# A build-time instruction plan that looks further along the product list, and counts waits in full from an earlier stage on

## The chip, the core and the metric

The kernel runs on one core of a Trainium2 chip. A core has TensorE (matrix products, "PE" in a profile; its weight loads are shown apart as "PEld"), VectorE ("DVE"), ScalarE ("ACT"), GpSimd ("POOL") and SyncE ("SP", which here only issues transfers), all reading one on-chip memory (SBUF); TensorE writes to eight accumulation banks (PSUM), from which VectorE and ScalarE fetch the results. The metric is the device time of one execution in microseconds, as a median of several runs.

## The reference, cut to what matters

A transformer block with linear attention and a gated feed-forward part, on 2048 tokens of width 1024, bf16 in and out:

```python
def _A_ref(x, wqkv, wo):                       # H = 32 heads of width 32
    q, k, v = split(x @ wqkv)
    phi = lambda t: jnp.where(t > 0, t + 1, jnp.exp(t)) + 1e-6
    pq, pk = phi(q), phi(k)
    kv = jnp.einsum("bhsd,bhse->bhde", pk, v)
    z = jnp.einsum("bhsd->bhd", pk)
    num = jnp.einsum("bhqd,bhde->bhqe", pq, kv)
    den = jnp.einsum("bhqd,bhd->bhq", pq, z)[..., None] + 1e-6
    return merge_heads(num / den) @ wo

def _B_ref(x, W_gate, W_up, W_down):           # F = 3584
    gate = x @ W_gate
    up = x @ W_up
    return (gate * (gate > 0) * up) @ W_down

h = x + _A_ref(_layernorm(x), wqkv, wo)
out = h + _B_ref(_layernorm(h), W_gate, W_up, W_down)
```

## The kernel before

Every large product is cut into quadrants and done with seven products in place of eight (Strassen-Winograd), so each has sums of inputs ahead of it and sums of results after it. `Quad` is one such group; its seven products are `p1` to `p7`, in the Q, K and V stages four matmuls of 128x512 each. `A`, `D` and `E` are PSUM banks.

```python
class Quad:
    def p1(self):
        self.A, self.D, self.E = self.banks()
        self.prod(self.A, 1, True)
        self.fork(self.D, self.A)                 # ScalarE copies the bank A to the bank D
    def p6(self):
        self.prod(self.A, 6, False)
        self.u2 = self.snap(self.A, 0)            # ScalarE copies A to SBUF
    def p5(self):
        self.prod(self.E, 5, True)
    def p7(self):
        self.prod(self.A, 7, False)
        self.u3 = self.snap(self.A, 1)
    def p2(self):
        self.prod(self.D, 2, False)
        self.out["c22"](self.E, self.u3)          # VectorE: E + u3; E is then free for p3
        self.out["c11"](self.D)
    def p4(self):
        self.prod(self.A, 4, False)
        self.out["c21"](self.A)
    def p3(self):
        self.prod(self.E, 3, False)
        self.out["c12"](self.E, self.u2)
```

In the Q and K stages a result goes through phi. `direct` takes a bank, `add` the sum of a bank and a copy, and `join2` ends the two sums together:

```python
        def direct(dst, k):
            def f(ps):
                nc.scalar.activation(out=e[:, k, :], in_=ps, func=ACT.Exp)
                phi_clamp(e[:, k, :])             # VectorE tensor_scalar, SBUF to SBUF
                phi_join(dst, ps, e[:, k, :])     # VectorE scalar_tensor_tensor, reads PSUM
            return f
        def add(k):
            return lambda E, u: nc.vector.tensor_tensor(out=c[:, k, :], in0=E, in1=u, op=ALU.add)
```

The attention of a tile of 128 tokens. `nd01` is groups 0 and 1, `nd2` group 2; all take turns on three PSUM banks (5, 6, 7), and so does `wo`:

```python
att = [ring_of([bank(b) for b in (5, 6, 7)])]
...
        def group(self, g):
            ...                                   # n = 3 or 2 heads' groups
            ps = att[0]()
            for k in range(n):
                nc.tensor.matmul(ps[:, k * NDW:(k + 1) * NDW], ...)        # 128x132
            ... nc.scalar.activation(Ln) ... nc.scalar.activation(Exp) ...
            nc.vector.tensor_tensor(out=self.o[...], in0=ndv[...], in1=rd[...], op=ALU.mult)
            if g == 2:
                self.oT = oT_ring()
                nc.sync.dma_start_transpose(out=self.oT, in_=self.o)
        def wo(self, j):
            ps = att[0]()
            for c in range(KC):                   # 8 matmuls of 128x512
                nc.tensor.matmul(ps, lhsT=self.oT[:, c, :], rhs=wo_sb[:, c, js], ...)
            nc.vector.scalar_tensor_tensor(out=self.h[:, js], in0=ps, ..., accum_out=self.acc[:, j:j + 1])
            if j == 1:
                return self.square                # then a ScalarE square, Ln, Exp, and
                                                  # nc.gpsimd.tensor_scalar(...) on 128x1024 of SBUF
```

The sums of the inputs of the gate and up products (VectorE, SBUF to SBUF, 128x1024) and of the left operand are work in the background:

```python
            return [sub(t[1], b[0][1], b[0][0]), sub(t[0], b[1][1], t[1]),
                    sub(t[2], b[1][1], b[0][1]), sub(t[3], b[1][0], t[0])]        # GW.sums
        return [tt(s1, a21, a22, ALU.add), tt(s2, s1, a11, ALU.subtract),
                tt(s4, a12, s2, ALU.subtract), tt(s3, a11, a21, ALU.subtract)]    # left_sums
```

None of this goes straight to the chip. `Plan` records every operation as a node (a run of matmuls into one bank is one node), works out what each depends on, and puts every engine's nodes in an order by a simulation at build time with its own estimates. `nom` is a TensorE node's place in the product list, in ns of TensorE work ahead of it; `late` is by when a node should start. The engines then run their lists strictly in the order that came out. The core of it:

```python
    WINDOW = 6000.0
    MIXED = (120000.0, 215000.0)                  # ns of the plan's own clock
    def schedule(self):
        ...
                if e == "tensor":
                    while first < len(pe) and pe[first] in done:
                        first += 1
                    limit = nodes[pe[first]].nom + self.WINDOW
                    a = [i for i in a if nodes[i].nom <= limit]
                s = max(clock[e], min(nodes[i].ready for i in a))
                if best is None or s < best[0]:
                    best = (s, e, a)
            ...
            s, e, a = best
            now = [i for i in a if nodes[i].ready <= s]
            i = min(now, key=lambda i: (nodes[i].nom if e == "tensor" else nodes[i].late, i))
            v = nodes[i]
            if e != "tensor":
                wait = (1.2 if self.MIXED[0] < s < self.MIXED[1] else 0.5) * v.hold
                soon = [j for j in a if s < nodes[j].ready < s + wait and nodes[j].late < v.late - 1500.0]
                if soon:
                    i = min(soon, key=lambda j: (nodes[j].late, j))
                    v = nodes[i]
                    s = v.ready
```

Of the kernel before, what the change touches and what calls it, by code (L numbers as in the profile page):

```python
# [32 lines left out]
class Plan:  # L33
# [3 lines left out]

    G = 64
    SEM = 100.0
    WINDOW = 6000.0  # L40
    AHEAD = 120000.0
    OPENING = 45000.0
    MIXED = (120000.0, 215000.0)

    class Node:
        __slots__ = ("eng", "calls", "preds", "hold", "lat", "open", "dma", "late", "ready", "left", "start", "nom")
# [156 lines left out]
    def schedule(self):  # L203
# [14 lines left out]
        while True:  # L218
            best = None
            for e in engines:  # L220
# [8 lines left out]
# [5 lines that stand above are left out]
# [11 lines left out]
# [4 lines that stand above are left out]
# [1325 lines left out]
```

## Time and profile before

| | before |
|---|---|
| time, median of 3 runs | 724.11 us (724.1 to 725.8) |
| profiled span | 722.2 us |
| TensorE busy | 713.6 us, 99% of the span |
| VectorE busy | 569.0 us, 79% |
| ScalarE busy | 277.9 us, 38% |
| GpSimd busy | 56.5 us, 8% |
| TensorE clock granted | 0.999 |

The stages, by the trace: to some 60 us the inputs, their norm and the first K and V groups; to 115 us the other K and V groups; to 200 us the Q groups, into which from 139 us the first half's attention and output projection are woven; to 285 us the first gate and up groups with the second half's attention; to 568 us the gate and up groups alone; then the down projection. The line number of nearly every instruction in the profile is 123, since the plan records and issues all of them from one place: an instruction is told by engine, operation and size. A matmul's busy time in the profile overlaps that of the next, so a row of matmuls without a gap shows as wholly busy, and short gaps hide in the overlap.

### The profile page before, as it was taken

What the parts mean: (1) busy time and instruction counts of PE and PEld (TensorE: products, weight loads), DVE (VectorE), ACT (ScalarE), POOL (GpSimd) and SP (SyncE); (2) the same over time, 40 slices, a digit from 0 to 9 for tenths busy, and PEclk for the clock granted to TensorE, in tenths of its full rate; (3) what the DMA queues carried; (4) which work ended last, traced back from release to release, by engine and by line L of the source; (5) the groups of instructions that cost most, each with busy time, mean ns of one, the idle gap of its engine ahead of it and who ended that gap; (6) DMA issues with size and microseconds to landing.
All of it is one profiled execution on the core that took longest, in us unless ns stands there. A gap on an engine that the chain in (4) does not pass through costs nothing.

```text
span 722.2 us, 11197 instructions
## 1 busy us (share of the span) xinstructions
PE 713.6 (99%) x4163; PEld 396.1 (55%) x4163; DVE 569.0 (79%) x966; ACT 277.9 (38%) x548; POOL 56.5 (8%) x62
## 2 busy tenths in 40 slices
PE   8999999999999999999999999999999999999998
PEld 3444445444454444444444444444444688888887
DVE  7899655888797975666766968769768879899996
ACT  5887555665655443333333333333333220001100
POOL 0000000012102120000000000000000004001452
PEclk9999999999999999999999999999999999999999
DMA  9556407069846630547145584685591878777974
GB/s 295 153 97 139 147 0 215 20 110 209 216 94 154 138 88 8 145 118 196 59 142 173 173 257 131 205 262 181 169 298 59 275 269 200 222 262 239 247 76 59
DMA packets 156503, 117.40 MB, mean 163 GB/s; under 512 B 54944, under 2 KB 140192, under 8 KB 156320
## 3 DMA queue, kind: packets, MB, share of 16 engines
q1 hardware_dynamic: 148832, 113.01, 54.1%
q0 software_dynamic: 7616, 3.67, 4.9%
q8 instruction: 32, 0.52, 0.3%
q14 instruction: 23, 0.19, 0.1%
HBM read 70.52 MB, written 34.08 MB: 145 GB/s over the span
## 4 chain that ended last, share of the span: by engine, by line
PE 87%; DVE 6%; ACT 3%; DMA 2%; issue 1%; SPq 0%; DVEq 0%; ACTq 0%
PE psum L123 87%; DVE mem L123 5%; ACT mem L123 2%; DMA mem<-mem 2%; DMA mem<-in_A_wqkv_dram 1%; DVE tiny L123 1%; ACT tiny L123 1%; SPq L123 0%; ACT psum L123 0%; DVEq L123 0%; ACTq L123 0%
## 5 line engine op out<-in xcount | busy, mean ns | idle before, releaser
L123 PE MATMUL psum<-mem 128*128 128x512 bf16 (+4 forms) x4147 | 712.7, 335 | 5.1 <-DVE mem L123 2.1
L123 PEld LDWEIGHTS <-mem 128*128 128x128 f16 (+1 forms) x4163 | 396.1, 98 | 322.4 <-issue 8.0
L123 DVE TENSOR_TENSOR mem<-psum,mem 128x512 f32<-128x512 f32 (+2 forms) x240 | 187.2, 793 | 97.3 <-ACT mem L123 64.7
L123 DVE TENSOR_TENSOR mem<-mem 128x512 f16<-128x512 bf16 (+8 forms) x400 | 241.2, 643 | 8.7 <-DMA mem<-mem 3.0
L123 ACT COPY mem<-psum 128x512 f32<-128x512 f32 (+2 forms) x124 | 92.7, 749 | 211.6 <-PE psum L123 205.5
L123 ACT COPY psum<-psum 128x512 f32<-128x512 f32 (+1 forms) x68 | 49.1, 722 | 157.8 <-PE psum L123 157.8
L123 POOL DMA_DIRECT2D out_dram<-mem x28 | 34.1, 1300 | 412.1 <-DVE mem L123 412.0
L123 ACT ACTIVATE mem<-psum 128x512 bf16<-128x512 f32 x90 | 53.5, 597 | 19.8 <-PE psum L123 19.2
L123 DVE SCALAR_TENSOR_TENSOR mem<-mem 128x512 bf16<-128x512 bf16 (+1 forms) x71 | 57.7, 812 | 1.2
L123 DVE SCALAR_TENSOR_TENSOR mem<-psum,mem 128x512 bf16<-128x512 f32 x66 | 45.4, 689 | 14.8 <-PE psum L123 12.5
L123 POOL TENSOR_SCALAR mem<-mem,tiny 128x1024 bf16<-128x1024 bf16 x16 | 20.7, 1296 | 243.0 <-ACT tiny L123 243.0
L123 ACT ACTIVATE mem<-mem,tiny 128x1024 bf16<-128x1024 bf16 x24 | 27.5, 1145 | 5.2 <-DVE tiny L123 5.0
L123 DVE TENSOR_SCALAR mem<-mem 128x512 bf16<-128x512 bf16 (+1 forms) x49 | 16.6, 340 | 15.3 <-ACT mem L123 15.1
L123 ACT ACTIVATE tiny<-tiny 128x1 f32<-128x1 f32 (+2 forms) x120 | 23.9, 205 | 7.5 <-DVE tiny L123 4.5
L123 ACT ACTIVATE mem<-mem 128x1024 bf16<-128x1024 f32 (+1 forms) x23 | 24.3, 1057 | 4.5 <-DVE mem L123 3.1
L123 DVE TENSOR_TENSOR mem<-psum,tiny 128x384 bf16<-128x384 f32 (+1 forms) x48 | 22.8, 507 | 4.1 <-ACT tiny L123 3.5
L123 ACT ACTIVATE tiny<-psum 128x12 f32<-128x12 f32 (+1 forms) x48 | 8.0, 170 | 18.5 <-PE psum L123 17.8
L123 DVE BATCH_NORM_STATS2 tiny<-mem 128x6 f32<-128x512 bf16 x16 | 10.3, 680 | 2.4 <-DMA mem<-in_A_x_dram 2.4
L123 ACT CAST mem<-psum 128x512 bf16<-128x512 f32 x18 | 10.3, 581 | 3.5 <-PE psum L123 3.2
L123 DVE TENSOR_SCALAR mem<-mem,tiny 128x1024 bf16<-128x1024 bf16 x16 | 8.6, 540 | 3.4 <-ACT tiny L123 3.3
L123 ACT ACTIVATION_READ_ACCUMULATOR mem<-mem,tiny 128x1 f32 x24 | 4.5, 188 | 0.0
L123 DVE TENSOR_SCALAR tiny<-tiny 128x1 f32<-128x1 f32 x16 | 3.4, 210 | 0.4
(17 smaller groups left out, 12.2 us busy)
## 6 DMA issues: line engine op xcount, KB each, us to landing
l_dram<-mem SPq DMA_DIRECT2D x98, 128.0 KB, 2.4
mem<-l_dram SPq DMA_DIRECT2D x12, 896.0 KB, 6.5
mem<-in_A_x_dram SPq DMA_DIRECT2D x32, 256.0 KB, 3.2
mem<-in_B_W_up_dram SPq DMA_DIRECT2D x14, 512.0 KB, 5.4
mem<-in_B_W_gate_dram SPq DMA_DIRECT2D x14, 512.0 KB, 4.4
mem<-in_B_W_down_dram SPq DMA_DIRECT2D x28, 256.0 KB, 3.5
r_dram<-mem SPq DMA_DIRECT2D x56, 128.0 KB, 2.4
mem<-r_dram SPq DMA_DIRECT2D x8, 896.0 KB, 5.3
```

The lines of the kernel that those rows point to most:

```text
L123: call = lambda: getattr(getattr(self.nc, eng), op)(*args, **k)
```

## The change

Two constants of the plan. `WINDOW` is how far beyond the first product not yet done TensorE may look for one that is ready, and `MIXED` the stretch of the plan's clock in which VectorE, ScalarE, GpSimd and SyncE may leave their engine waiting up to 1.2 times the length of the operation at hand (0.5 times elsewhere) when a more urgent one is about to be ready. The first is to find products that fill TensorE's waits, the second is to let urgent evictions go first in the K and V stage too. No operation is added, removed or changed; only the orders differ.

```diff
     G = 64
     SEM = 100.0
-    WINDOW = 6000.0
+    WINDOW = 10000.0
     AHEAD = 120000.0
     OPENING = 45000.0
-    MIXED = (120000.0, 215000.0)
+    MIXED = (62000.0, 215000.0)
```

Built, the two programs have the same 4163 matmuls. What the orders show, in the names above:

- VectorE, from the earlier start of `MIXED` alone: in four K groups the sum `c22` (E + u3) comes ahead of the `c11` join, not behind it; in the group at 82 us it also comes ahead of two `left_sums`; two or three more neighbours swap. TensorE's order doesn't change from this.
- TensorE, from `WINDOW` alone, output projection stage: before, each round is `wo` (8 matmuls), `nd2` (2), `wo` (8), `nd01` (6), one product of a Q group (4). After, one Q product is put ahead of the first `wo`, so that each round has the Q product that stood one round later, and the last of them (`p4`) no longer stands between the last `wo` pairs. VectorE's work follows: the 128x1024 `sub`s of `GW.sums`, one in each of four rounds before, begin two rounds later.
- TensorE, from `WINDOW`, at 205 us: `p5` of the second gate/up half group and `p3` of the first come ahead of `p6` of the second. And at 570 us, in the first group of the down projection, `p1` of its second half comes ahead of `p1` of its first half.
- A few transfers and background sums from 400 us on change places.

## The prediction

> **What bounds the kernel now.** I read the page's busy times first, then busy times by stage, then the list of TensorE's waits, and last the timeline around each wait.
>
> ```profile
> span 722.2 us, 11197 instructions
> ...
> PE 713.6 (99%) x4163; PEld 396.1 (55%) x4163; DVE 569.0 (79%) x966; ACT 277.9 (38%) x548; POOL 56.5 (8%) x62
> ...
> L123 PE MATMUL psum<-mem 128*128 128x512 bf16 (+4 forms) x4147 | 712.7, 335 | 5.1 <-DVE mem L123 2.1
> ```
>
> TensorE is the bound, and only 5.1 us of idle time stand before its matmuls. But the 335 ns are overlapped records, so I need the true pitch. By stage (columns: stretch, its length, then busy time and count by engine):
>
> ```profile
> 147.00:183.00 36.00, 34.49 (x193) 16.75 (x191) 29.07 (x70) 20.30 (x71) 7.16 (x6) 1.00 0.85 176
> ...
> 285.00:560.00 275.00, 275.00 (x1276) 124.48 (x1274) 202.35 (x347) 92.06 (x115) 0.00 (x0) 1.00 0.56 169
> ```
>
> From 285 to 560 us there are 1276 matmuls of 128x512 in 275 us: 215.5 ns each, and no wait. A single record of that size lasts 380 ns. So whenever the timeline shows TensorE idle for g before a matmul, g + (0.380 - 0.216) = g + 0.16 us is lost; a gap under 0.16 doesn't show at all. Its waits:
>
> ```profile
> PE psum L123 <- DVE mem L123: 2.1, 5, 0.9
> ...
> PE psum L123 <- DMA mem<-mem: 0.8, 1, 0.8
> ...
> PE psum L123 <- ACT psum L123: 0.2, 1, 0.2
> ```
>
> I went through the start of every matmul in the trace and summed what goes beyond its pitch. Up to 60 us it is 3.7 us (warm-up and first inputs; no order changes there). From 60 us on the whole of it is 4.1 us, in twelve gaps: 0.07 at 67.3, 0.32 at 68.5, 0.55 at 82.1, 0.14 at 147.4, 0.94 at 149.6, 0.21 at 164.2, 0.51 at 169.4, 0.51 at 174.7, 0.16 at 192.3, 0.39 at 205.6, 0.20 at 267.4, and 0.10 at 572.6 hidden in the overlap. That is the most an order can bring: 4.1 of 724 us, 0.6%. The change can't reach 2% on the fast side.
>
> **What the Trainium skill says.** "TensorE: Matmul & The Clock Gate", "Step-by-step: what each phase is for", gives the back-to-back gap as N/2.4 GHz plus about 2.5 ns, 216 ns at N=512; the trace agrees (215.5). "Perfetto Trace Analysis", "Tensor Engine Instruction (MATMUL, LD_WEIGHTS)", says the end of a matmul is an estimate and that ScalarE, VectorE and GpSimd are strict FIFOs; hence the gaps from starts, and hence an eviction stuck behind whatever VectorE's list has ahead of it. "SBUF — State Buffer", "SBUF: two separate sides", says that a VectorE operation with two SBUF inputs and a GpSimd operation lock each other out of a shared port for a whole instruction. The trace agrees: the same 128x1024 sub takes 1.15 us at 162.3, 167.6 and 172.9, each time over a GpSimd operation of 1.19 us, and 0.68 us at 175.7 without one.
>
> **The change part by part.** No operation is added or removed, so the sum is over gaps alone.
>
> *K stage, from the earlier start of the full waits.* VectorE's order ahead of the gap at 82.1:
>
> ```profile
> 78.95 1.56 DVE L123 TENSOR_TENSOR mem<-mem 128x512 f16<-128x512 bf16 x4 [1.70 <-DMA mem<-mem]
> 80.42 0.29 DVE L123 TENSOR_SCALAR mem<-mem 128x512 bf16<-128x512 bf16 x1
> 80.75 0.69 DVE L123 SCALAR_TENSOR_TENSOR mem<-psum,mem 128x512 bf16<-128x512 f32 x1
> 81.36 0.68 DVE L123 TENSOR_TENSOR mem<-psum,mem 128x512 f32<-128x512 f32 x1
> ```
>
> ```profile
> 82.09 1.24 PE L123 MATMUL psum<-mem 128*128 128x512 bf16 x5 [0.38 <-DVE mem L123]
> ```
>
> The last VectorE line is c22, which frees E for p3. The new order puts it ahead of the join (0.69) and of two or three of the four sums (about 0.39 each). Its other input, the copy u3, is done at 80.60 (ScalarE, 80.02 + 0.58), so it can run from 80.65 to 81.33; p3 was due at 82.09 - 0.55 = 81.54. The gap goes: -0.55. At 68.5 the same swap moves c22 from 67.79 up to about 67.36 (u3 is done at 67.30): it ends at 68.04, p3 is due at 68.20: -0.32. From 83 to 147 us TensorE has no wait, and what is moved back (left sums that the next group needs from 90 us on) has over 4 us to spare, so nothing gives this back. Part sum -0.87.
>
> *The gap at 149.6.* TensorE waits for the DMA transpose of the first attention tile:
>
> ```profile
> 149.57 19.52 PE L123 MATMUL psum<-mem 128*128 128x512 bf16 x112 [0.78 <-DMA mem<-mem]
> ```
>
> A Q product of 4 x 0.216 = 0.86 us goes into this gap of 0.94. It needs only the fork of its bank (ScalarE, done at 147.85), so it starts at 148.63 and ends at 149.49: -0.86, paid out at 181.7, where the product then is no longer in the way.
>
> *The gaps at 164.2, 169.4, 174.7.* Each `wo` takes the bank of the `wo` before it, and waits for that eviction:
>
> ```profile
> 172.33 1.19 POOL L123 TENSOR_SCALAR mem<-mem,tiny 128x1024 bf16<-128x1024 bf16 x1 [4.09 <-ACT tiny L123]
> 172.57 0.42 DVE L123 TENSOR_TENSOR mem<-psum,tiny 128x256 bf16<-128x256 f32 x1 [0.45 <-ACT tiny L123]
> 172.91 1.15 DVE L123 TENSOR_TENSOR mem<-mem 128x1024 f16<-128x1024 bf16 x1
> ...
> 173.99 0.68 DVE L123 SCALAR_TENSOR_TENSOR mem<-psum,mem 128x512 bf16<-128x512 f32 x1
> ...
> 174.72 7.62 PE L123 MATMUL psum<-mem 128*128 128x512 bf16 x36 [0.34 <-DVE mem L123]
> ```
>
> The product in the bank was done at about 173.17, but VectorE had begun a background sub, stretched to 1.15 by GpSimd, and evicts only at 173.99. In the new order the first such sub comes two rounds later: the gaps at 164.2 and 169.4 (0.21 and 0.51) go. Ahead of the `wo` now at 174.7 the sub is there again, with a 1.22 us join before it, so a gap of 0.2 (as at its first time before) to 0.5 stays: I put 0.35. After that `wo` follows `wo`, whose banks were free long before, and no sub is in the way. Part sum 1.23 - 0.35 = -0.88. Against it: with the last Q product gone from 181.7, the last `wo` pair starts 5.2 us after the group it needs (1.73 x 3), and the way there was 1.7 us (group to transpose issue at 178.31) plus 3.1 to 3.5 (median to landing, and the longest near it): +0.1.
>
> *The gap at 205.6.* p6 waits for ScalarE's fork, which stood behind a Relu:
>
> ```profile
> 204.42 0.60 ACT L123 ACTIVATE mem<-psum 128x512 bf16<-128x512 f32 x1 [0.34 <-DVE mem L123]
> ...
> 204.92 0.59 ACT L123 COPY psum<-psum 128x512 f32<-128x512 f32 x1
> ...
> 205.56 7.65 PE L123 MATMUL psum<-mem 128*128 128x512 f16 x42 [0.23 <-ACT psum L123]
> ```
>
> p5 needs the Relu alone (205.02), and was due at 205.17. But p3, now next at 206.03, needs two small sums that end near 206.1 to 206.2: -0.25 of the 0.39. At 572.6 the half product put ahead takes the hidden gap: -0.1. The gaps at 147.4, 192.3 and 267.4 stay: the last two come from VectorE behind a GpSimd operation, which moves with them.
>
> Sum: -0.87 - 0.86 - 0.88 + 0.1 - 0.25 - 0.1 = -2.86 us. I take 0.25 off for gaps that I don't see: -2.6, so 721.5 us.
>
> **Rivals.** (1) VectorE bounds the output projection, and the filled gap comes back as longer waits: 29.07 of 36 us busy from 147 to 183. For it speaks that every wait there but one ends with VectorE; against it that VectorE itself idles 7 us there, and that the moved work finds lighter rounds. Then the 0.86 and much of the 0.88 are lost: about 723.2. (2) The urgent-first waits leave VectorE idle in the K stage and push sums or the norm late, so that a later group's p6 or p5 waits: VectorE is busy 31.3 of 40 us from 60 to 100, and the moved sums are due 4 us later, so I give this little; it would make 723.5 to 724.5. (3) The transfers and sums that change places from 400 us on open a new gap in the last stage, where VectorE has 19.8 of 20 us busy from 660 to 700 and TensorE waits for nothing only because all of it comes just in time: one load that is late by its whole way (5.3 to 6.5 us median to landing for the large ones) would make 727. Speaks against it: none of TensorE's products after 590 us moves, and only neighbours swap.
>
> **Range and chances.** All gaps gone but none new: 720.7. Only the K stage and half of the rest: 722.9. The before's own runs reach 1.7 above their median, so I widen up: 720.6 to 723.3. For 2% it would have to be under 709.6 or over 738.6: the first is out of reach, the second takes a new stall of 14 us.
>
> **What would show it.** Starts of p3 without a gap at 68 and at about 81.5; no idle before a Q product at 148.6; TensorE's idle after DVE down from 2.1 to about 1.2 (0.9 at 29 us, and one gap left ahead of the `wo` now at 174.7); p5 at about 202.5 (205.2 less the gain) and at its pitch; as many matmuls by 285 as before, 2.7 us earlier; no wait at all after. Wrong if gaps near 160 to 180 sum to over 1 us still, or if TensorE waits for a transfer after 560 us.

## Result, and the profile after

| | before | changed | ratio, with its 95% interval |
|---|---|---|---|
| time, median, first comparison | 724.23 us (723.78 to 725.8, 6 runs) | 722.27 us (721.18 to 723.02, 6 runs) | 0.9968 (0.9955 to 0.9981) |
| time, median, second comparison | 724.49 us (724.09 to 724.97, 10 runs) | 722.01 us (721.55 to 722.77, 6 runs) | 0.9967 (0.9955 to 0.9979) |
| profiled span | 722.2 us | 719.9 and 720.1 us | |

The change takes 0.3% off: 0.0032 x 724.23 = 2.3 us, with an interval of 1.4 to 3.3 us. (The ratio is that of the means; the medians differ by 1.96 us in the first comparison and by 2.48 in the second.) That is far under 2%, and the 722.27 us lie within the predicted 720.6 to 723.3. The page of the changed kernel (span; then busy time, share of the span and count by engine):

```profile
span 719.9 us, 11145 instructions
...
PE 710.4 (99%) x4112; PEld 396.6 (55%) x4163; DVE 568.1 (79%) x966; ACT 278.2 (39%) x548; POOL 57.3 (8%) x62
```

Busy times outside TensorE are within 1 us of those of before (VectorE 568.1 for 569.0); no operation was changed, so what can have changed is TensorE's waits. One trap stands in the PE figure: x4112. The kernel has 4163 matmuls, as the weight loads (PEld x4163) show, so 51 records are missing from this trace. Each leaves a false gap of one pitch, 0.215 us, in front of the next matmul. I leave those out below. A second profile of the same kernel has all 4163, and I use it where counts matter. Its TensorE from 66 to 183 us (start, length, operation, count; the timeline begins a new line where TensorE was idle):

```profile
65.73 117.56 PE L123 MATMUL psum<-mem 128*128 128x512 bf16 x646
```

One line. In the kernel before, the same stretch has six, broken at 68.52, 82.09, 149.57, 169.44 and 174.72. Its busy times by stage (stretch, length, busy time and count of PE, PEld, DVE, ACT, POOL; granted clock, DMA share, GB/s):

```profile
60.00:100.00 40.00, 40.00 (x232) 19.98 (x230) 31.98 (x58) 26.53 (x52) 0.00 (x0) 1.00 0.47 112
147.00:183.00 36.00, 35.90 (x201) 17.63 (x201) 29.51 (x72) 21.53 (x70) 7.16 (x6) 1.00 0.85 184
```

From 147 to 183 us TensorE does 201 matmuls where it did 193: 8 x 0.2155 = 1.72 us. VectorE's busy time there rose only from 29.07 to 29.51. And TensorE's waits in the first profile of the changed kernel (us in total, times, longest):

```profile
PE psum L123 <- DVE mem L123: 1.1, 1, 1.1
PE psum L123 <- ACT mem L123: 0.7, 1, 0.7
```

Against before: the wait for a DMA (0.8) and the one for ScalarE's bank copy (0.2) are gone, and of five waits for VectorE (2.1 us) one is left, the one near 29 us, where the order didn't change; shorter ones hide in the overlap or stand under "issue".

As in the prediction, I took the start of every matmul and summed what goes beyond its pitch, place by place (us lost, at the time of before; "again" is the second profile of the changed kernel; the last column belongs to an experiment below):

| place | before | changed | changed, again | `MIXED` to 300000 |
|---|---|---|---|---|
| 67.3 | 0.07 | 0.07 | 0.07 | 0.07 |
| 68.5, K stage | 0.32 | 0 | 0 | 0 |
| 82.1, K stage | 0.55 | 0 | 0 | 0 |
| 147.4 | 0.14 | 0.14 | 0.14 | 0.14 |
| 149.6, transpose | 0.94 | 0.07 | 0.06 | 0 |
| 164.2, `wo` | 0.21 | 0 | 0 | 0 |
| 169.4, `wo` | 0.51 | 0 | 0 | 0 |
| 174.7, `wo` | 0.51 | 0.27 | 0.27 | 0.27 |
| 181, last `wo` pair | 0 | 0 | 0 | 0.08 |
| 192.3 | 0.16 | 0 | 0.36 | 0 |
| 205.6 | 0.39 | 0.20 | 0.20 | 0.20 |
| 213.6, `nd2` (new) | 0 | 0.29 | 0.21 | 0 |
| 267.4 | 0.20 | 0.20 | 0.21 | 0 |
| 572.6 | 0.10 | 0.10 | 0.10 | 0.10 |
| sum | 4.10 | 1.34 | 1.61 | 0.85 |

The orders win 2.76 us in one profile and 2.49 in the other. Of this the spans show 2.3 and 2.1: up to 60 us, where the order is the same, the changed kernel's profiles lose 4.19 and 4.18 us and that of before 3.78. The account is complete: the span less the loss before 60 us and the loss after it is 714.3 to 714.4 us in the profile of before and in all ten others below, so nothing but these gaps makes the spans differ. I come back to the opening under what I hadn't expected.

The main gaps, line by line, in the first profile of the changed kernel. VectorE near 81 us (timeline: start, length, operation; in brackets idle time and what ended it):

```profile
79.87 0.29 DVE L123 TENSOR_SCALAR mem<-mem 128x512 bf16<-128x512 bf16 x1
80.72 0.69 DVE L123 TENSOR_TENSOR mem<-psum,mem 128x512 f32<-128x512 f32 x1 [0.56 <-ACT mem L123]
81.32 0.68 DVE L123 SCALAR_TENSOR_TENSOR mem<-psum,mem 128x512 bf16<-128x512 f32 x1
```

The second line is `c22`. VectorE now waits 0.56 us for the copy that `c22` needs, and does the join afterwards. `c22` starts at 80.72 where it started at 81.36, so the bank for `p3` is free in time. That idle 0.56 us is the meaning of "counts waits in full".

The `wo` at 173 us (same view; the last line is TensorE's weight load for it):

```profile
170.90 1.19 POOL L123 TENSOR_SCALAR mem<-mem,tiny 128x1024 bf16<-128x1024 bf16 x1 [3.59 <-ACT tiny L123]
...
171.48 1.15 DVE L123 TENSOR_TENSOR mem<-mem 128x1024 f16<-128x1024 bf16 x1
...
172.56 0.68 DVE L123 SCALAR_TENSOR_TENSOR mem<-psum,mem 128x512 bf16<-128x512 f32 x1
...
173.30 0.74 PEld L123 LDWEIGHTS <-mem 128*128 128x128 bf16 x4 [0.38 <-issue]
```

The pattern of before in its one place left: a background `sub` of 1.15 us stretched over GpSimd's 1.19, the eviction behind it, and the `wo` behind the eviction, 0.27 us late.

And the gap that no step of the prediction had, at 213.6 us:

```profile
211.69 0.69 DVE L123 SCALAR_TENSOR_TENSOR mem<-mem 128x512 bf16<-128x512 bf16 x1
212.29 0.69 DVE L123 TENSOR_TENSOR mem<-mem 128x1024 f16<-128x1024 bf16 x1
...
212.89 0.69 DVE L123 SCALAR_TENSOR_TENSOR mem<-psum,mem 128x512 bf16<-128x512 f32 x1
...
213.64 1.29 PEld L123 LDWEIGHTS <-mem 128*128 128x128 bf16 x8 [0.41 <-issue]
```

`nd2` needs the bank of a `wo` whose product ends at 212.30. At 212.29 VectorE had just begun a background `sub`; the eviction comes 0.6 us later, and `nd2` starts at its end.

### The profile page after: what moved, and what is told of

The parts are those of the page before. It is cut to its first block, busy times and chain, and to the rows that moved or that the text cites. A ratio compares the mean times of both kernels' runs of the same rounds, so it can differ in the third digit from the quotient of the medians.

```text
span 719.9 us, 11145 instructions
## 1 busy us (share of the span) xinstructions
PE 710.4 (99%) x4112; PEld 396.6 (55%) x4163; DVE 568.1 (79%) x966; ACT 278.2 (39%) x548; POOL 57.3 (8%) x62
## 4 chain that ended last, share of the span: by engine, by line
PE 94%; DVE 3%; DMA 2%; issue 1%; ACT 0%; SPq 0%; DVEq 0%; ACTq 0%
PE psum L123 94%; DVE mem L123 2%; DMA mem<-in_A_wqkv_dram 1%; DMA mem<-mem 1%; SPq L123 0%; DVE tiny L123 0%; ACT mem L123 0%; ACT tiny L123 0%; DVEq L123 0%; ACTq L123 0%
```

## The experiments

My theory: the gain is the sum of the gaps that each constant closes, the two parts are independent, and what is left (173, 213.6, 265 us) is VectorE having begun something else when an urgent eviction came due. Rivals: the waits cost something elsewhere in the K stage; the moves of the window after 200 us undo part of its gain; GpSimd has nothing to do with the gap at 173. In each diff the left side is the kernel named.

**1. The waits alone (against before).**

```diff
-    MIXED = (120000.0, 215000.0)
+    MIXED = (62000.0, 215000.0)
```

> The early start of the full waits alone (WINDOW back at 6000). My theory, that the two parts add: the gaps at 68.5 and 82.1 us (0.32 and 0.55 before) are gone as in the changed kernel, all later ones stay as before (0.94 at 149, 0.21, 0.51 and 0.51 from 163 to 175, 0.39 at 205), TensorE loses 4.10 - 0.87 = 3.2 us after 60 us, ratio 0.9988. The rival, that VectorE's waiting is paid for later: the same two gaps are gone but a new one of some 0.5 to 0.9 us opens by 115 us, ratio 1.000.

Measured: ratio 0.9984 (0.9977 to 0.9991), 723.81 against 724.73 us. TensorE's waits in its profile:

```profile
PE psum L123 <- DVE mem L123: 1.4, 3, 0.7
...
PE psum L123 <- DMA mem<-mem: 0.8, 1, 0.8
...
PE psum L123 <- ACT psum L123: 0.2, 1, 0.2
```

Five waits for VectorE became three; the other two stand as before. By the matmul starts the gaps at 68.5 and 82.1 are gone, all others are within 0.01 us of before, and none is new: 4.10 to 3.23 us, 0.87 as the prediction worked out. The rival of sums pushed late in the K stage falls.

**2. The window alone (against before).**

```diff
-    WINDOW = 6000.0
+    WINDOW = 10000.0
```

> WINDOW 10000 alone (full waits from 120000 again). My theory: gaps of 0.32 and 0.55 at 68 and 82 us as before; 149.6 falls from 0.94 to 0.07, 164 and 169 go, about 0.27 is left near 174, 205 falls from 0.39 to 0.20, and the new 0.29 near 214 is there, since it comes from this part: 4.10 - 1.9 = 2.2 us lost after 60 us, ratio 0.9974. The rival, that the window's gain needs the earlier K stage (the two don't add): about half, with longer gaps near 164 to 175, ratio 0.9985.

Measured: 0.9978 (0.9969 to 0.9987), 723.27 us. The gaps of the K stage are there (0.32 and 0.54), and the changed kernel's gaps after it: 0.08 at 150.1, 0.26 at 174.3, 0.20 at 205.0, 0.17 at 214.7; 0.19 stands at 191.1. Sum 2.27 us, so 1.83 of the 4.10 are won. Both parts together: 0.87 + 1.83 = 2.70 us of gaps, against 2.76 and 2.49 for the whole change; 0.0016 + 0.0022 = 0.0038 by the ratios, against 0.0032 with an interval that holds it. The parts add up. The new gap belongs to the window.

**3. The full waits also after 215000 (against the changed kernel).** The new gap looks like those that the full waits removed in the K stage, so I let them go on.

```diff
-    MIXED = (62000.0, 215000.0)
+    MIXED = (62000.0, 300000.0)
```

> The changed kernel with the full waits kept up to 300000 of the plan's clock in place of 215000. Theory: the new gap of 0.29 us at 213.6 and the 0.20 at 265.0 are evictions and sums for freed banks that stand behind background sums of 128x1024, because the full waits end just ahead of them; with the waits kept on, both go and nothing else moves: 1.34 - 0.49 = 0.85 us lost after 60 us, ratio to before 0.9962 to 0.9953. Rival: the gaps come from GpSimd's hold on the shared port or from the moved products, and are still there (sum over 0.4 us), ratio as the changed kernel, 0.9968.

Measured: 0.9952 (0.9940 to 0.9965), 721.44 us. VectorE at the place of the new gap:

```profile
211.55 0.69 DVE L123 TENSOR_TENSOR mem<-mem 128x1024 f16<-128x1024 bf16 x1
212.60 0.69 DVE L123 SCALAR_TENSOR_TENSOR mem<-psum,mem 128x512 bf16<-128x512 f32 x1 [0.36 <-PE psum L123]
```

VectorE waits 0.36 us for the product and evicts it at once. TensorE has no gap there, nor at 265. The sum after 60 us is 0.85 us, as expected. TensorE's order is that of the changed kernel; only VectorE's and ScalarE's differ, from about there on. So the cause of the new gap is shown by its removal: the background work that VectorE had begun.

**4. Short GpSimd operations (against the changed kernel, same order).** This kernel leaves work out: the 16 GpSimd operations at the end of the second norm do 128 of their 1024 columns.

```diff
-call = lambda: getattr(getattr(self.nc, eng), op)(*args, **k)
+call = lambda: getattr(getattr(self.nc, eng), op)(*args, **(
+    {**k, "out": k["out"][:, 0:128], "in0": k["in0"][:, 0:128]}
+    if (eng, op) == ("gpsimd", "tensor_scalar") else k))
```

> The changed kernel in the very same order, but the 16 GpSimd operations that end the second norm do 128 of 1024 columns (the rest of each normed row stays unnormed: work is left out). Theory of the shared port: the 128x1024 subs of the projection stage, 1.15 us over a GpSimd operation, all take 0.68 to 0.75; the gap of 0.27 us near 173.3 goes (the eviction starts 0.4 earlier), and the 0.20 near 265 goes; the 0.29 near 213.6 stays, since no GpSimd operation is near it. Rival, that the long subs come of the transfers (DMA share 0.85 there) or of reading bf16 strided: subs stay at 1.1 to 1.2 and both gaps stay.

Measured: 0.9962 (0.9948 to 0.9976), 722.15 us. Its timeline at the `sub` of 173 us, and TensorE after it:

```profile
171.37 0.45 POOL L123 TENSOR_SCALAR mem<-mem,tiny 128x128 bf16<-128x128 bf16 x1 [4.33 <-DVE mem L123]
...
171.89 0.68 DVE L123 TENSOR_TENSOR mem<-mem 128x1024 f16<-128x1024 bf16 x1
...
172.49 0.68 DVE L123 SCALAR_TENSOR_TENSOR mem<-psum,mem 128x512 bf16<-128x512 f32 x1
```

```profile
180.81 3.41 PE L123 MATMUL psum<-mem 128*128 128x512 bf16 x15 [0.18 <-DMA mem<-mem]
```

The same `sub` in the same place of the list takes 0.68 in place of 1.15 us, and the gap at 173 is gone, so GpSimd's length is its cause. The gap at 265 is gone too: two `sub`s that take 2.12 us over a GpSimd operation in the changed kernel take 1.28 here. (In experiment 3 that gap went with GpSimd at its full length, because the second of these `sub`s was not begun; it takes both.) The gap at 213.6 stays, at 0.20 us. But TensorE now waits 0.34 us for the last transpose at 180.8: it landed 3.95 us after its issue, in the changed kernel 3.20. Sum 1.12 us.

**5. The window at the output projection only (against the changed kernel).** From 188000 ns of the product list on, the old 6000 hold.

```diff
-limit = nodes[pe[first]].nom + self.WINDOW
+limit = nodes[pe[first]].nom + (self.WINDOW if nodes[pe[first]].nom < 188000.0 else 6000.0)
```

> The changed kernel, but TensorE looks 10000 ahead only while the first product not done lies in the first 188000 of the list, and 6000 after that: the moves of the output projection stay, those at 205 and 570 us are undone. Theory: 149, 164, 169 as in the changed kernel (0.07, 0, 0, and 0.27 near 173); the fork's gap near 203 is back at 0.39 and the 0.16 near 190 too; the new 0.29 near 213.6 shrinks or goes, since VectorE's list there is that of before. Sum 1.4 to 1.6 us after 60 us, against 1.34: the moves at 205 and 570 brought next to nothing, ratio 0.9969. Rival, that the moves at 205 carry their 0.25 us: sum 1.7 or more, ratio 0.9973.

Measured: 0.9965 (0.9951 to 0.9978), 722.28 us. TensorE at 204 us:

```profile
204.49 11.82 PE L123 MATMUL psum<-mem 128*128 128x512 f16 x67 [0.23 <-ACT psum L123]
```

The gap of 0.39 of before is back, and the one at 213.6 is gone: one line from 204.49 to 216.31. So the move of `p5` and `p3` ahead of `p6` wins 0.19 us at once and costs 0.17 to 0.29 us ten us later (the profiles of experiments 2 and 4 and the two of the changed kernel). Its net is about nothing. The whole sum is 1.66 us, just over the expected 1.4 to 1.6 and just under the rival's 1.7; of it 0.18 is a wait for the last transpose and 0.24 the gap at 191.2, places that differ between profiles anyway. The time can't tell this kernel from the changed one.

**6. Further still (against the changed kernel).**

```diff
-    WINDOW = 10000.0
+    WINDOW = 20000.0
```

> The changed kernel with WINDOW 20000. Theory: only one product's worth of wait was there to fill at 149 us, so looking further only pulls more forward: a second Q product ahead of the first output projection delays it by some 0.8 us without a gap to fill, p6 near 203 comes without anything ahead of its fork (gap of 0.3 to 0.6), sum after 60 us 1.3 to 2.0 us, ratio 0.9968 to 0.9980: no better than 10000. Rival, the further the better: sum under 1.0 us, ratio 0.9960 or less.

Measured: 0.9983 (0.9974 to 0.9991), 723.65 us: nearly half of the gain is lost, which I had not expected. Two Q products now go ahead of the first `wo`. The gap at 149 is wholly gone, but those at 169.8 (0.26) and 175.1 (0.51) are back, and there is one of 0.77 at 203.7:

```profile
203.05 0.55 DVE L123 TENSOR_TENSOR mem<-psum,tiny 128x384 bf16<-128x384 f32 x1
...
203.65 4.68 PE L123 MATMUL psum<-mem 128*128 128x132 bf16 x28 [0.61 <-DVE mem L123]
```

`nd01` (the 128x132 matmuls) waits for VectorE, which reads an earlier group's bank (the 128x384 operation) only at 203.05, behind a join of 1.22 us. Sum 2.40 us. I expected 1.3 to 2.0.

**7. The full waits from 20000 on (against the changed kernel).** The largest gap of all is near 29 us, before `MIXED` begins.

```diff
-    MIXED = (62000.0, 215000.0)
+    MIXED = (20000.0, 300000.0)
```

> Full waits from 20000 to 300000 of the plan's clock (WINDOW 10000). Theory: the gap near 29 us (0.7 to 1.5 in the profiles so far) is the same case as that at 82, a bank's sum c22 behind a join of 0.69, so it shrinks by about 0.7; the rest as with waits to 300000 (0.9 after 60 us): ratio 0.994 to 0.9955. Rival, that in the first 60 us transfers set the pace and the wait only moves to a later product of the same stage: loss before 60 us still 3.8 to 4.6, ratio 0.9952 to 0.9965.

Measured: 0.9953 (0.9940 to 0.9965), 721.78 us. The gap near 29 us is gone, and TensorE has this instead:

```profile
55.78 14.47 PE L123 MATMUL psum<-mem 128*128 128x512 bf16 x77 [0.68 <-DVE mem L123]
```

0.84 us lost at 55.8, and 0.21 in place of 0.07 at 68.1. The loss before 60 us is 4.5 us, within the rival's 3.8 to 4.6: as the rival said, the wait only moves to a later product of the same stage. Its reason, that transfers set the pace, is not shown: this wait ends with VectorE's `c22`, ahead of which stand four sums of 128x512 (1.55 us from 53.38). Whether VectorE has too much to do there, or again a poor order, stays open.

**8 and 9. The changed kernel and number 3 once more, side by side.** No edits.

> The changed kernel as it is, beside the next run on one chip, to see whether the end of MIXED at 300000 is worth anything over the change itself. Both hold the same order up to about 205 us. Theory (the gaps at 213.6 and 265 are real losses, 0.5 us together): this one 0.4 to 0.6 us slower than the next run, at a ratio to before near 0.9960; its gap at 213.6 is there again (0.2 to 0.3 us). Rival (the 0.5 us lie within the scatter of the opening, and the lower time of the first look at 300000 was luck): the two medians within 0.2 us.

> The changed kernel with the end of MIXED at 300000, again, beside the run before it. Theory: 0.4 to 0.6 us under the changed kernel, ratio to before 0.9950 to 0.9956; no gap at 213.6 nor at 265, the gaps after 60 us sum to 0.9 us where the changed kernel has 1.3. Rival: within 0.2 us of it.

Measured: 722.01 us (721.55 to 722.77) at 0.9967 (0.9955 to 0.9979), and 721.64 us (721.23 to 722.52) at 0.9962 (0.9949 to 0.9974). The gaps at 213.6 and 265 are there in number 8 (0.21 and 0.21) and absent in number 9; the sums are 1.61 and 1.18 us. So by trace the longer waits are worth 0.43 us here and 0.49 us between the first profiles. The medians differ by 0.37 us, under the 0.4 to 0.6 of the theory and over the 0.2 of the rival, and the intervals overlap. It beats the kernel before in both comparisons; that it beats the changed kernel is shown by the traces and not by the times.

## Why the prediction was right

The prediction was 721.5 us, 0.9964 of its 724.11; measured were 0.9968 and 0.9967. Step by step:

- **K stage, -0.87: right.** Both gaps went, experiment 1 alone gives 0.87, and `p3` of the 82 us group starts 0.47 us earlier than before in a profile whose first 60 us were 0.40 us slower: 0.87 again.
- **The gap at 149.6, -0.86: right.** 0.07 and 0.06 are left where the sum said 0.08.
- **The `wo` gaps, -0.88: right in mechanism, 0.08 too cautious.** Those at 164.2 and 169.4 went; the one left is 0.26 to 0.27 in every kernel with `WINDOW` at 10000 that has it, where I put 0.35 between 0.2 and 0.5. Experiment 4 shows the cause that the prediction read from four durations.
- **"Against it: ... the last `wo` pair ... +0.1": right as a risk, and not a constant.** No wait in either profile of the changed kernel, but 0.08, 0.18 and 0.34 us in experiments 3, 5 and 4. The transpose decides it: TensorE is ready for this pair 3.43 to 3.44 us after the transpose's issue (3.65 in experiment 4), and the transpose lands after 3.20 us in both profiles of the changed kernel, but after 3.48, 3.56 and 3.95 in those three. The prediction took 3.5 for the longest near it; in the trace of before, one issued at 173.02 took 4.19.
- **205.6, -0.25: right in mechanism; it was 0.19.** `p5` no longer waits, and `p3` waits for two small sums, as written. The step "that end near 206.1 to 206.2" was mis-sized by 0.06.
- **572.6, "the half product put ahead takes the hidden gap", -0.1: wrong.** 0.10 stays in every profile, with the move and, in experiment 5, without it. One half product lies between `p1` and the product that needs its copy in both orders; the move changes which, and not how much time the copy has.
- **"The gaps at 147.4, 192.3 and 267.4 stay": right for the first and the last; 192.3 is not a constant.** It was 0.16 before, 0 and 0.36 in two profiles of the same changed program; the reason is below.
- **What no step had: 0.29 (again: 0.21) at 213.6.** I looked at what the moved products at 205 us gain, and not at which eviction falls behind which background `sub` ten us later. It uses up the 0.25 "for gaps that I don't see". Nor did I ask what lies just after the end of `MIXED`; experiment 3 shows that this is where it sits.
- **The total: in part luck.** In the first profile the other misses cancel: 0.08 at the `wo`, 0.10 at the last pair and 0.16 at 192.3 on the good side, 0.06 at 205.6 and 0.10 at 572.6 on the other, and the new gap. So 2.76 us won stand against the 2.86 of the sum. In the second, the 0.36 at 192.3 makes it 2.49.
- **The range has a slip.** "Only the K stage and half of the rest: 722.9" doesn't follow from its own terms: 0.87 and half of the other 1.99 would give 722.2. The upper end of 723.3 was widened by the scatter of the runs, and nothing else rests on it.

The rivals. Rival 1, VectorE bounding the projection, would have brought the filled time back as longer waits: it did not, with 201 matmuls in the 36 us for 193. In experiment 6, with one product more in the gap, two of the waits did come back, but not because VectorE had more to do (29.59 us in these 36): a `sub` of 1.15 us, begun at 167.98 and at 173.26 over a GpSimd operation, stands ahead of the evictions at 169.05 and 174.34, as it did before. Rival 2 falls with experiment 1. Rival 3 did not come: there is no gap after 573 us in any profile, and the matmul that has 1477 ahead of it, at 285.09 us before, is at 283.00 in the second profile of the changed kernel: the 2.49 us won less the 0.40 of the opening. The same 2.09 us are still there at 700 us.

## What to carry to other kernels

When one engine is busy to 99%, list every gap of it from the starts of its instructions, with the overlap taken out: the sum is the most that an order can bring, and each gap's closing can be worked out from what the engine before it does in the microsecond ahead. Then look not only at the gaps that a change fills but at what the moved work pushes in front of the next urgent result, just past the end of the changed stretch. A constant that is better at 10000 than at 6000 need not be better still at 20000.

## What was not expected

**The same program, two outcomes of one race.** At 190 us a VectorE clamp (128x512, SBUF to SBUF) and a GpSimd operation come due together. In the first profile of the changed kernel, and then in the second:

```profile
187.39 1.29 DVE L123 TENSOR_TENSOR mem<-mem 128x1024 f16<-128x1024 bf16 x2
...
187.99 1.87 POOL L123 TENSOR_SCALAR mem<-mem,tiny 128x1024 bf16<-128x1024 bf16 x1 [3.08 <-ACT tiny L123]
...
188.59 0.29 DVE L123 TENSOR_SCALAR mem<-mem 128x512 bf16<-128x512 bf16 x1
```

```profile
187.68 0.69 DVE L123 TENSOR_TENSOR mem<-mem 128x1024 f16<-128x1024 bf16 x1
...
187.99 1.45 POOL L123 TENSOR_SCALAR mem<-mem,tiny 128x1024 bf16<-128x1024 bf16 x1 [3.06 <-ACT tiny L123]
...
188.41 1.18 DVE L123 TENSOR_SCALAR mem<-mem 128x512 bf16<-128x512 bf16 x1
...
190.23 2.97 PE L123 MATMUL psum<-mem 128*128 128x512 f16 x13 [0.20 <-DVE mem L123]
```

Once the GpSimd operation is the long one (1.87 against its usual 1.19) and the clamp takes its 0.29; once the clamp takes 1.18, and TensorE loses 0.36 us. "SBUF — State Buffer", "SBUF: two separate sides", of the Trainium skill says that whichever of the two starts first holds the shared port for its whole instruction, and that a VectorE operation in a two-port mode is concerned as well as one with two SBUF inputs. The clamp has one SBUF input, and the trace agrees that it can be held up. The prediction had used the page for the `sub`s only.

What differs is how far VectorE's `sub`s had come. In the first profile they end at 188.68, when the clamp's input is already there (ScalarE, 187.80 + 0.58 = 188.38), and VectorE goes from one straight into the other. In the second they end at 188.37, just when that input comes, and the GpSimd operation, begun at 187.99, seems to have got the port in between: it ends at 187.99 + 1.45 = 189.44, and the clamp at 189.59. The other profiles with GpSimd operations of full length fit: in experiment 3's the work ahead of the clamp ends 0.04 us after the input, and the clamp takes 0.29; in the remaining seven (before among them) it ends 0.04 to 0.41 us ahead of the input, and the clamp takes 0.92 to 1.14. With the short operation of experiment 4 it takes 0.39. So less than 0.1 us of VectorE's progress can decide it. That it is the port for which they compete fits all eleven profiles, but no run here tests that alone. The ten profiles of kernels with the wider window or the earlier waits show 0 to 0.36 us here.

**The opening varies more than the changes differ.** Up to 60 us the order is the same in all kernels here except experiment 7, and yet the time lost there is 3.78 us in the one profile of before, and 4.18 to 5.14 us in nine others. Two places make it up. In the first 10 us the loss is 2.6 us in before and 2.7 to 3.7 in the others: the first matmuls start 0.427 us apart in place of 0.2155, up to 4.2 us in before and up to 4.2 to 6.7 in the others. From 25 to 32 us it is 1.2 us in before and 0.7 to 1.95 in the others; the gap near 29 alone goes from 0.72 to 1.5. What sets either, and whether before is lower there by chance, stays open. A difference of 0.4 us between two profiles can't be read without taking this stretch out.

**The wait for the last transpose** went from nothing to 0.34 us between kernels with the same `wo` order, with the time in which that transpose landed (3.20 to 3.95 us). It differs within one program too: 3.48 us in experiment 3 and 3.35 in experiment 9, with a wait of 0.08 and none. Why one lands later than another stays open.
